# A table of single moves on top of a planned instruction order, in a fused hash-masked attention and mixture-of-attention kernel

## The chip, the cores and the metric

The kernel runs on one core of a Trainium2 chip. The metric is the device time of one execution in microseconds (us), as the median over the runs of the kernel. Beside these runs one execution was recorded by the hardware profiler; its span is the time from its first to its last instruction.

## The reference, cut to what matters

Two stages follow each other. The first is an attention over 4 batches, 8 heads, 768 tokens and 64 dimensions, in which a query sees only the keys whose six sign bits (the signs of a projection) are its own. The second is a mixture of four causal attention heads over the first stage's output, with the two largest gate logits of a token as its weights.

```python
q_bits = (np.einsum('bhsd,dk->bhsk', q, proj) > 0); k_bits = (np.einsum('bhsd,dk->bhsk', k, proj) > 0)
mask = q_bucket[:, :, :, None] == k_bucket[:, :, None, :]
scores = np.where(mask, scale * np.matmul(q, k.transpose(0, 1, 3, 2)), -1e9)
attn = np.exp(scores - np.max(scores, -1, keepdims=True))
x = np.matmul(attn / (np.sum(attn, -1, keepdims=True) + 1e-09), v)      # -> [4, 768, 512]
logits = x @ w_gate                                                     # top 2 of 4, softmax over the two
for e in range(4):                                                      # q = x @ wq[e], k = x @ wk[e], v = x @ wv[e]
    scores = np.where(causal, -1e9, scale * (q @ k.transpose(0, 2, 1)))
    a = softmax(scores)
    out += weight_of_e * (a @ v @ wo[e])
```

## The kernel before

The work consists of 48 units: 32 heads of the first stage (each batch has 8) and 16 of the second (4 for each batch). A unit goes through the same steps each time. `max_steps` multiplies queries and keys on TensorE into tiles named `mx`, and VectorE reduces each to row maxima (`pm`; `pmw` for the first four heads, which use a wider fp32 path). `shift_steps` turns the maxima into a row that is put under the queries by a DMA: `negm` or `negh` on VectorE, a transposition into `misc` on TensorE, then a copy `roww` or `row`, and for the hash heads `fr`, which a DMA puts into `fq`. `s_unit` then goes over pieces of 128 keys by up to 512 queries: `qk` multiplies into `st` (two matmuls a tile) and ScalarE takes the exponential twice, as fp32 `p32` (`p` in the profile's rows) and as fp16 `ph`; `lo` takes `pl` = `p32` - `ph` on GpSimd; `av` multiplies `ph` by `vh`, `ph` by `vl` and `pl` by `vh` into `o`. At the end of a hash head three or more matmuls `o<-vs,fq` close the sum, and `normalise` divides it (`rden`, its reciprocal, `xp`). `prep_v` makes `vf` and `vh` on ScalarE and `vl` on GpSimd, and adds up columns of them with matmuls `misc<-ones,vh` and `misc<-ones,vl`. Other jobs load inputs, find signs and scales, split operands into two fp16 parts (the instructions SCALAR_TENSOR_TENSOR `qk<-natq` and `qk<-natk` on VectorE), project for the second stage and write the output.

Buffers are rings: three PSUM tiles `st`, two `mx`, two `misc`, one `o`; four `p32`, seven `ph`, five `pl`. A tile is used again when its readers are through.

No instruction is issued where it is written. A recorder notes all 10,944 operations with what each depends on; `schedule` then places them one by one on their engines, by planned durations (`TIMES`), latencies and priorities (a table `PLACE` shifts the priority of each job on each engine). In the planned waits of TensorE during the opening it sets dummy matmuls `o<-ident`. `issue` issues the list in its order: each engine carries out its own instructions in the order in which they were issued, and waits by semaphores for what the next one needs. An operation may have two alternatives (a copy on ScalarE or VectorE). A field `after` gives a GpSimd operation one wait more, for a VectorE operation on which it does not depend; `schedule` sets it where the plan has both at the same time. All instructions of the profile thus carry one line number, that of the call in `issue` (L735).

Of the kernel before, what the change touches and what calls it, by code (L numbers as in the profile page):

```python
# [141 lines left out]
LAT = {"tensor": 55.0, "scalar": 36.0, "vector": 37.0, "gpsimd": 78.0, "sync": 28.0}  # L142
LAT2 = {"tensor": 55.0, "scalar": 103.0, "vector": 100.0, "gpsimd": 132.0, "sync": 28.0}
LAT_PE = {"gpsimd": 174.0}


PLACE = [
# [315 lines left out]
class Recorder:  # L463
# [103 lines left out]
    def schedule(self):  # L567
# [14 lines left out]
        def after(p, e, many):  # L582
            if p.eng == e:
                return p.end + SAME[e]
            return p.end + (LAT_PE[e] if e in LAT_PE and many and p.eng == "tensor" else (LAT2 if many else LAT)[e])

# [15 lines left out]
        order = []  # L602
# [8 lines left out]
        while left:  # L611
# [41 lines left out]
            st, o, a, pen = best  # L653
# [66 lines left out]
                    enter(p)  # L720
            order.append((o, a))
        self.length = max(o.end for o in self.ops)
        return order

    def issue(self):
        def real(x):
# [1201 lines left out]
```

## Time and profile before

| | before |
|---|---|
| median of 3 runs | 605.97 us (605.92 to 608.73) |
| the profiled execution, its own time | 606.81 us |
| its span | 605.0 us |
| mean granted clock of TensorE | 0.999 of full speed |
| instructions | 20,583 |

The page names the engines PE (TensorE), PEld (its weight loads, which overlap PE), DVE (VectorE), ACT (ScalarE), POOL (GpSimd) and SP (the engine that issues most DMAs). Matmuls overlap each other: a row's duration is that of one matmul from start to end, while the next may start much earlier. A busy engine is therefore not the same as an engine at its peak. Idle time stands in brackets in a row, with the instruction that ended it.

### The profile page before, as it was taken

What the parts mean: (1) busy time and instruction counts of PE and PEld (TensorE: products, weight loads), DVE (VectorE), ACT (ScalarE), POOL (GpSimd) and SP (SyncE); (2) the same over time, 40 slices, a digit from 0 to 9 for tenths busy, and PEclk for the clock granted to TensorE, in tenths of its full rate; (3) what the DMA queues carried; (4) which work ended last, traced back from release to release, by engine and by line L of the source; (5) the groups of instructions that cost most, each with busy time, mean ns of one, the idle gap of its engine ahead of it and who ended that gap; (6) DMA issues with size and microseconds to landing.
All of it is one profiled execution on the core that took longest, in us unless ns stands there. A gap on an engine that the chain in (4) does not pass through costs nothing.

```text
span 605.0 us, 20583 instructions
## 1 busy us (share of the span) xinstructions
PE 591.0 (98%) x7911; PEld 434.0 (72%) x7911; DVE 503.2 (83%) x1383; ACT 497.6 (82%) x1060; POOL 465.6 (77%) x520
## 2 busy tenths in 40 slices
PE   8999999999999999999999999999999999999996
PEld 7677876767777677777766777777776677776673
DVE  5899979999879898977979988888998967557753
ACT  6588999999679998968988798976987997943783
POOL 9478898999658899867895889974894889931740
PEclk9999999999999999999999999999999999999999
DMA  6564053141320433131234224123051210002222
GB/s 183 141 190 126 9 167 110 43 149 40 107 61 16 143 91 76 36 113 28 94 102 133 83 47 120 29 95 72 20 165 73 76 29 23 10 1 64 62 89 105
DMA packets 32921, 50.26 MB, mean 83 GB/s; under 512 B 6411, under 2 KB 20535, under 8 KB 32823
## 3 DMA queue, kind: packets, MB, share of 16 engines
q1 hardware_dynamic: 32810, 48.95, 28.0%
q8 instruction: 62, 1.02, 0.7%
q14 instruction: 37, 0.29, 0.2%
q10 hardware_dynamic: 12, 0.00, 0.0%
HBM read 20.98 MB, written 6.29 MB: 45 GB/s over the span
## 4 chain that ended last, share of the span: by engine, by line
PE 82%; ACT 8%; DVE 3%; POOL 2%; issue 2%; DMA 1%; SPq 0%; ACTq 0%; DVEq 0%; POOLq 0%
PE misc L735 24%; PE st L735 24%; PE o L735 22%; PE mx L735 12%; ACT ph L735 3%; ACT p L735 3%; POOL pl L735 2%; DVE pm L735 1%; DVE qk L735 1%; DMA qk<-qk 1%; DMA wst<-in_wvg_dram 1%; ACT vf L735 0%; ACT qk L735 0%; DVE xt L735 0%; POOL vl L735 0%
## 5 line engine op out<-in xcount | busy, mean ns | idle before, releaser
L735 POOL TENSOR_TENSOR pl<-p,ph 128x512 f16<-128x512 f32 x367 | 411.2, 1148 | 115.5 <-ACT ph L735 49.7
L735 ACT ACTIVATE p<-st 128x512 f32<-128x512 f32 x372 | 225.7, 608 | 34.8 <-PE st L735 28.3
L735 PE MATMUL st<-qk 78*128 78x512 f16 (+3 forms) x976 | 228.1, 323 | 1.0 <-ACT ph L735 0.7
L735 ACT ACTIVATE ph<-st 128x512 f16<-128x512 f32 x372 | 224.1, 611 | 2.3 <-PE o L735 2.0
L735 DVE TENSOR_REDUCE pm<-mx 128x2 f32<-128x512 f32 (+2 forms) x284 | 186.0, 675 | 16.9 <-PE mx L735 15.2
L735 PEld LDWEIGHTS <-ph 128*128 128x128 f16 x2880 | 160.2, 98 | 24.6 <-issue 1.0
L735 PEld LDWEIGHTS <-qk 78*128 78x128 f16 (+5 forms) x1560 | 129.5, 98 | 55.2 <-issue 5.3
L735 PEld LDWEIGHTS <-pl 128*128 128x128 f16 x1440 | 133.1, 97 | 10.5 <-POOL pl L735 2.2
L735 PE MATMUL mx<-qk 76*128 76x512 f16 (+2 forms) x488 | 134.7, 323 | 2.4 <-DVE pm L735 1.1
L735 PE MATMUL o<-vh,ph 128*128 128x65 f16 x1104 | 128.9, 195 | 0.3 <-DVE xp L735 0.2
L735 PE MATMUL o<-vl,ph 128*128 128x64 f16 x1104 | 128.3, 193 | 0.8 <-POOL vl L735 0.8
L735 PE MATMUL o<-vh,pl 128*128 128x65 f16 x1104 | 128.3, 194 | 0.1
L735 PE MATMUL misc<-xt,wqk_h 128*128 128x384 f16 x256 | 57.7, 325 | 0.3 <-DVE qk L735 0.3
L735 DVE CUSTOM_DVE_ANT_0 spare<-mx,causal 128x512 bf16<-128x512 f32 (+2 forms) x96 | 44.3, 461 | 6.4 <-PE mx L735 4.1
L735 PEld LDWEIGHTS <-xt 128*128 128x128 f16 x324 | 30.5, 97 | 11.2 <-ACT xt L735 0.5
L735 PE MATMUL o<-mvh,pl 128*128 128x65 f16 x336 | 37.6, 193 | 0.5 <-POOL pl L735 0.5
L735 PE MATMUL o<-mvh,ph 128*128 128x65 f16 x336 | 37.6, 194 | 0.0
L735 PE MATMUL o<-mvl,ph 128*128 128x64 f16 x336 | 37.5, 192 | 0.0
L735 POOL TENSOR_TENSOR vl<-vf,vh 128x384 f16<-128x384 f32 x32 | 30.1, 948 | 7.0 <-ACT vh L735 3.5
L735 PEld LDWEIGHTS <-wqk_h 128*128 128x128 f16 x256 | 23.9, 98 | 14.2 <-issue 0.7
L735 PE MATMUL misc<-xt,wqk_l 128*128 128x384 f16 x128 | 29.9, 325 | 0.0
L735 PE MATMUL misc<-wvg_h,xt 128*128 128x260 f16 x192 | 29.4, 274 | 0.0
(198 smaller groups left out, 890.9 us busy)
## 6 DMA issues: line engine op xcount, KB each, us to landing
qk<-qk SPq DMA_DIRECT2D x128, 96.0 KB
natv<-in_v_dram SPq DMA_DIRECT2D x16, 384.0 KB
qk<-qk SPq DMA_DIRECT2D x32, 192.0 KB
natq<-in_q_dram SPq DMA_DIRECT2D x15, 384.0 KB
natk<-in_k_dram SPq DMA_DIRECT2D x15, 384.0 KB
out_dram<-ot SPq DMA_DIRECT2D x20, 256.0 KB
wst<-in_wqk_dram SPq DMA_DIRECT2D x4, 256.0 KB
xt<-xt SPq DMA_DIRECT2D x4, 192.0 KB
```

The costliest lines, as they stand in the source:

```text
L735: o.made = getattr(getattr(self.nc, e), m)(*[real(x) for x in args], **{k: real(x) for k, x in kw.items()})
```

## The change

The changed kernel has three tables more and a method `moved`, through which `schedule` sends its finished list. `MOVES` has 3,501 entries `i:p`: operation `i` is taken out of its place and put right behind operation `p`. `SWAPS` lists 37 operations which take their other alternative: 23 copies go from VectorE to ScalarE, 13 from ScalarE to VectorE, and one `pl` from VectorE to GpSimd. One of them stands in the first 127 us, the copy `vr` at 49.47 us. `BEHIND` replaces the planner's own 27 `after` waits of GpSimd by 21 others. The operations themselves, the tiles, the rings and the dummy matmuls are the same.

```diff
+MOVES = """
+5:9 13:5 17:13 15:17 2:6 18:8 20:12 19:14 23:22 66:30 31:66 43:31 134:33 3:134
...
+SWAPS = (481, 2075, 2308, 2255, 2459, 2523, 3066, 4379, 4559, 4645, 4807, 4875, 4887, 4938, 5410, 5695, 6259, 6468, 6894, 6835, 7064, 7531, 7599, 8248, 9032, 8
...
+BEHIND = """
+797:372 386:388 935:833 1105:863 2002:1776 2043:1806 2509:2511 2786:2559 3279:3227 3429:3238 5012:4507 4654:4523 5261:5252 5368:5263
...
@@ -720,7 +980,41 @@
         self.length = max(o.end for o in self.ops)
-        return order
+        return self.moved(order)
+
+    def moved(self, order):
+        first, at = {}, {}
+        for x in MOVES.split():
+            i, p = map(int, x.split(":"))
+            at[p] = i
+        gone = set(at.values())
+        swaps = set(SWAPS)
+        for o in self.ops:
+            o.after = None
+        for x in BEHIND.split():
+            i, p = map(int, x.split(":"))
+            self.ops[i].after = self.ops[p]
+        for o, a in order:
+            if o.i >= 0 and o not in first:
+                first[o] = a
+        ops = {o.i: (o, next(b for b in o.alts if b is not a) if o.i in swaps else a) for o, a in first.items()}
+        out, seen, p = [], set(), -1
+        while p in at:
+            p = at[p]
+            out.append(ops[p])
+        for o, a in order:
+            if o.i < 0 or o.i in seen:
+                out.append((o, a))
+                continue
+            seen.add(o.i)
+            if o.i in gone:
+                continue
+            p = o.i
+            out.append(ops[p])
+            while p in at:
+                p = at[p]
+                out.append(ops[p])
+        return out
```

Most moves are short. On TensorE 1,584 of 7,643 operations leave the order in which they stood to each other, nine in ten of its operations stand within 9 places of where they stood, and the first 20 us of its program are as before. On VectorE 186 operations leave that order, on ScalarE 305, on GpSimd 84 and on SP 114. Three places follow. The first is VectorE's program from about 9 to 22 us, around the first head's maxima (`pmw`), its `fr`, and the four sign instructions `xt<-misc,least_times` of the first head pair. Before:

```order
L735 TENSOR_REDUCE pmw_183<-mx 128x2 x9
L735 TENSOR_REDUCE negm_163<-pmw_183 128x12
L735 TENSOR_SCALAR fr<-misc 12x128
L735 TENSOR_SCALAR xt<-misc,least_times 13x384 x2
L735 TENSOR_SCALAR xt<-misc,least_times 12x384 x2
L735 TENSOR_REDUCE mx<-pst 128x1
L735 TENSOR_REDUCE mx<-natv 128x1
```

The same stretch of VectorE's program after the change:

```order
L1029 TENSOR_REDUCE pmw_172<-mx 128x2 x8
L1029 TENSOR_REDUCE mx<-pst 128x1
L1029 TENSOR_REDUCE pmw_172<-mx 128x2
L1029 TENSOR_REDUCE negm_147<-pmw_172 128x12
L1029 TENSOR_SCALAR xt<-misc,least_times 12x384
L1029 TENSOR_SCALAR xt<-misc,least_times 13x384 x2
L1029 TENSOR_SCALAR xt<-misc,least_times 12x384
L1029 TENSOR_SCALAR fr<-misc 12x128
L1029 TENSOR_REDUCE mx<-natv 128x1
```

The four sign instructions now stand ahead of `fr`, and `mx<-pst` stands further up. On SP's queue the DMA `fq<-fr` stays ahead of a load of `natv` and of two weight loads, which change places with each other behind it.

The second place is GpSimd's program from about 40 to 49 us, with the pair of `vl` that belongs to the next head (`x2`) and the `pl` around it. Before:

```order
L735 TENSOR_TENSOR vl_718<-vf_265,vh_257 128x6x64
L735 TENSOR_TENSOR pl<-p_915,ph 128x512
L735 TENSOR_TENSOR pl<-p_929,ph 128x512
L735 TENSOR_TENSOR pl<-p_943,ph 128x512
L735 TENSOR_TENSOR vl_981<-vf_268,vh_260 128x6x64 x2
L735 TENSOR_TENSOR pl<-p_1005,ph 128x512
```

After the change (buffer numbers differ, since tiles are numbered in the order of issue):

```order
L1029 TENSOR_TENSOR vl_703<-vf_261,vh_270 128x6x64
L1029 TENSOR_TENSOR pl<-p_919,ph 128x512
L1029 TENSOR_TENSOR pl<-p_931,ph 128x512
L1029 TENSOR_TENSOR vl_980<-vf_170,vh_197 128x6x64 x2
L1029 TENSOR_TENSOR pl<-p_945,ph 128x512
L1029 TENSOR_TENSOR pl<-p_992,ph 128x512
```

The pair of `vl` now stands ahead of the third `pl`.

The third place is VectorE's program from about 47 to 52 us, between the end of a head (`rden` to `xp`) and a maximum over a weight tile (`qkmax<-wst`). Before:

```order
L735 TENSOR_REDUCE pmw_185<-mx 128x2 x2
L735 TENSOR_SCALAR rden<-o,cs_590 128x6
L735 TENSOR_REDUCE qkmax<-wst 128x2
L735 RECIPROCAL rden<-rden 128x6
L735 TENSOR_TENSOR vr_235<-misc,vr_235 1x128
L735 TENSOR_TENSOR xp<-o,rden 128x6x64
L735 TENSOR_REDUCE pmw_185<-mx 128x2 x2
```

And after the change:

```order
L1029 TENSOR_REDUCE pmw_176<-mx 128x2 x2
L1029 TENSOR_SCALAR rden<-o,cs_590 128x6
L1029 CAST vr_257<-misc 1x128
L1029 RECIPROCAL rden<-rden 128x6
L1029 TENSOR_TENSOR vr_257<-misc,vr_257 1x128
L1029 TENSOR_TENSOR xp<-o,rden 128x6x64
L1029 TENSOR_REDUCE pmw_176<-mx 128x2 x2
L1029 TENSOR_REDUCE mqk<-natq 128x1
L1029 TENSOR_REDUCE mqk<-natk 128x1
L1029 TENSOR_REDUCE pmw_176<-mx 128x2
L1029 TENSOR_REDUCE qkmax<-wst 128x2
```

`qkmax<-wst` has gone behind `xp` and five other reductions; the copy `vr`, one of the 37, has come over from ScalarE.

## Rows read from the trace of the kernel before

**Rows 1.** The page: busy time and share of each engine; shares of the last chain.

```profile
PE 591.0 (98%) x7911; PEld 434.0 (72%) x7911; DVE 503.2 (83%) x1383; ACT 497.6 (82%) x1060; POOL 465.6 (77%) x520
...
PE 82%; ACT 8%; DVE 3%; POOL 2%; issue 2%; DMA 1%; SPq 0%; ACTq 0%; DVEq 0%; POOLq 0%
```

**Rows 2.** Windows: stretch and length, busy us (instructions) per engine, clock, DMA share, GB/s.

```profile
0.00:50.00 50.00, 45.11 (x492) 35.13 (x493) 40.22 (x87) 34.86 (x78) 36.27 (x113) 1.00 0.60 173
50.00:100.00 50.00, 48.58 (x714) 37.86 (x713) 45.70 (x108) 46.90 (x98) 44.77 (x40) 1.00 0.32 97
```

**Rows 3.** Windows again, one stretch of 20 us; engines PE, PEld, DVE, ACT, POOL.

```profile
80.00:100.00 20.00, 19.08 (x262) 13.79 (x260) 19.26 (x41) 20.00 (x43) 18.09 (x18) 1.00 0.49 159
```

**Rows 4.** Timeline of PE: start, duration, form, count, idle time before and its releaser.

```profile
1.83 0.61 PE L735 MATMUL o<-ident 128*128 128x128 bf16 x4 [1.83 <-DVE ident L735]
...
17.20 2.40 PE L735 MATMUL o<-ident 128*128 128x128 bf16 x40
20.21 0.70 PE L735 MATMUL mx<-xt 76*128 76x512 f32 x3 [0.62 <-DVE xt L735]
...
46.53 0.27 PE L735 MATMUL o<-vs,fq 80*128 80x65 f16 x3
47.66 0.18 PE L735 MATMUL misc<-ones,vl 128*128 128x1 f16 x1 [0.86 <-POOL vl L735]
...
50.62 0.19 PE L735 MATMUL o<-vh,ph 128*128 128x65 f16 x1 [0.22 <-DVE xp L735]
...
61.69 0.38 PE L735 MATMUL st<-qk 77*128 77x256 f32 x1 [0.19 <-ACT ph L735]
...
89.23 0.38 PE L735 MATMUL st<-qk 78*128 78x512 f16 x1 [0.16 <-ACT ph L735]
...
399.67 0.32 PE L735 MATMUL mx<-qk 65*128 65x384 f16 x1 [0.46 <-DVE pm L735]
...
554.87 0.59 PE L735 MATMUL mx<-qk 65*128 65x512 f16 x2 [1.04 <-DMA qk<-qk]
...
600.33 0.38 PE L735 MATMUL o<-wo_h,xt 128*128 128x512 f16 x1
```

**Rows 5.** Timeline of DVE at the three places and at one split of keys.

```profile
17.70 0.28 DVE L735 TENSOR_SCALAR fr<-misc 12x128 f16<-12x128 f32 x1 [1.50 <-ACT roww L735]
18.01 2.76 DVE L735 TENSOR_SCALAR xt<-misc,least_times 13x384 fp32r<-13x384 f32 x4
...
43.81 1.00 DVE L735 SCALAR_TENSOR_TENSOR qk<-natk,cs,qk 128x768 f16<-128x768 f32 x1
...
48.38 1.21 DVE L735 TENSOR_REDUCE qkmax<-wst 128x2 f32<-128x1024 f32 x1
...
50.03 0.53 DVE L735 TENSOR_TENSOR xp<-o,rden 128x384 f32<-128x384 f32 x1
...
64.47 1.25 DVE L735 SCALAR_TENSOR_TENSOR qk<-natq,cs,qk 128x768 f16<-128x768 f32 x1
```

**Rows 6.** Timeline of ACT and of SP's queue at the first and second place.

```profile
44.31 0.97 ACT L735 ACTIVATE vh<-vf 128x384 f16<-128x384 f32 x2
...
18.00 0.77 SPq L735 DMA_DIRECT2D fq<-fr  x1
18.83 0.41 SPq L735 DMA_DIRECT2D natv<-in_v_dram  x1
```

**Rows 7.** Timeline of POOL at the second place, and beside the split of rows 5.

```profile
41.57 4.26 POOL L735 TENSOR_TENSOR pl<-p,ph 128x512 f16<-128x512 f32 x3 [0.38 <-ACT ph L735]
45.80 1.81 POOL L735 TENSOR_TENSOR vl<-vf,vh 128x384 f16<-128x384 f32 x2
...
63.75 2.99 POOL L735 TENSOR_TENSOR pl<-p,ph 128x512 f16<-128x512 f32 x2
```

**Rows 8.** Waits up to 100 us: who, for whom, total us, times, longest.

```profile
PEld st L735 <- ACT ph L735: 2.3, 7, 0.6
```

**Rows 9.** The page's costliest groups: the subtraction on POOL, with its mean in ns.

```profile
L735 POOL TENSOR_TENSOR pl<-p,ph 128x512 f16<-128x512 f32 x367 | 411.2, 1148 | 115.5 <-ACT ph L735 49.7
```

More of the change, by code (lines that the diff above doesn't have):

```diff
@@ L144 @@
 LAT_PE = {"gpsimd": 174.0}
+MOVES = """
[251 rows of a table added]
+"""
+SWAPS = (481, 2075, 2308, 2255, 2459, 2523, 3066, 4379, 4559, 4645, 4807, 4875, 4887, 4938, 5410, 5695, 6259, 6468, 6894, 6835, 7064, 7531, 7599, 8248, 9032, 8772, 9351, 10196, 9912, 10354, 10381, 10472, 10697, 10786, 10907, 10912, 10942,)
+BEHIND = """
+797:372 386:388 935:833 1105:863 2002:1776 2043:1806 2509:2511 2786:2559 3279:3227 3429:3238 5012:4507 4654:4523 5261:5252 5368:5263
+5955:5959 6610:6596 6684:6612 7463:7247 8438:7976 8679:8726 10786:10780
+"""
 PLACE = [
```

250 rows, old and new, of the table MOVES are left out of this document.

## Prediction

> **What bounds the kernel now.** I read the page first, then windows, then PE's timeline, and last the engines that PE waits for. PE is busy 591.0 us of a span of 605.0, and the chain that ended last is PE for 82% of it [rows 1]. No work is removed, and nearly all that is moved keeps its engine, so the change can only win time in which PE stands still, or in which two matmuls follow each other later than they could.
>
> Two bounds for that. The windows give the time without any matmul: 4.89 us in the first 50 us and 1.42 in the next 50 [rows 2]; over the whole span it is 605.0 - 591.0 = 14.0 [rows 1]. Of it 1.83 lies before the first matmul, which waits for VectorE's `ident`, and some 4.3 behind the last, which starts at 600.33 and takes 0.38 [rows 4]; the change leaves both parts alone. So 7.9 us are idle inside. The busy column hides more, since matmuls overlap: a matmul that starts 0.2 us late is covered by the end of the one before. I therefore took the distance from each matmul's start to the next one's, for all 7911 from 1.83 to 600.33 [rows 4], less the median distance of the same shape: 166 of them are over 0.04 us too long, 24.8 us in sum. 13 are over 0.4 us (8.6 us together), the other 153 add up to 16.2, of which 11.1 lie in the first 100 us.
>
> **The change part by part.** The sum is made against the profiled execution's 606.81 us, that is the span and 1.81 around it; the median of the runs, 605.97, is 0.84 lower, and I take that off at the end.
>
> *First place, PE's 0.62 us ahead of 20.21.* PE runs dummies from 17.20 for 2.40 us, to 19.60, and then waits for VectorE's signs [rows 4]. VectorE has nothing to do for 1.50 us before `fr`, which waits for ScalarE's `roww`; the four signs stand behind `fr` and run from 18.01 for 2.76 us [rows 5]. Now they stand ahead. They can begin at 17.70 - 1.50 = 16.20 at the earliest, and at 17.70 at the latest; three of them take about 2.07, so PE can go on between 18.3 and 19.8, where it is free at 19.60. Gain 0.62, at least 0.4; more is not there, as the dummies stay. What is late next: `fr` by some 2 us, and with it the DMA `fq<-fr`, at 18.00 on SP's queue, and `natv` behind it at 18.83 [rows 6], which the weight loads also pass. `fq` is first read at 46.53 [rows 4], the head pair's `vh` comes at 44.31 [rows 6]: over 20 us of cover, so nothing.
>
> *Second place, 0.86 us ahead of 47.66.* PE's `misc<-ones,vl` waits for the pair of `vl` [rows 4], which GpSimd starts at 45.80, after three `pl` from 41.57 to 45.83 [rows 7]. ScalarE's two `vh` are ready at about 44.8 and 45.28 [rows 6]. With only two `pl` ahead (2 of 1.15 us [rows 9], to about 43.9) the pair begins at 44.8 and is done 1.81 later, at 46.6 to 46.7. PE comes there right after 46.53 and its two steps, at 46.66. All 0.86 goes; if the signs' 0.62 makes PE come earlier but not `vh`, as little as 0.4 does. The third `pl` ends at about 47.9 in place of 45.8, still ahead of the `o` matmuls from 50.62 [rows 4].
>
> *Third place, 0.22 us ahead of 50.62.* PE waits for `xp` [rows 4]; `qkmax` (1.21 us) ran before it [rows 5] and now comes after, while the copy `vr` comes in between. A copy of one row I take at the 0.28 of `fr` [rows 5]. So `xp` is some 0.9 earlier and the 0.22 goes (0 if `rden`'s own input is the limit).
>
> *Small named ones.* Ahead of 61.69 and 89.23 PE waits 0.19 and 0.16 for ScalarE's `ph` [rows 4]; its program has now a matmul that was ready in front of each: 0.35 (0 to 0.35). Ahead of 399.67 it waits 0.46 for a maximum on VectorE [rows 4], which has moved up a little: 0.26 (0 to 0.46).
>
> *What stays.* The 1.04 us before 554.87 is a chain of a copy, a DMA and its landing [rows 4], whose order is the same.
>
> *The 153 small steps.* Those named above take 1.0 of their 16.2 us. Of the other 15 I take a fifth as gone, 3.0, because about a fifth of PE's operations (1,584 of 7,643) change places with neighbours; bounds 0, as a neighbour need not be ready earlier, and 7.5, half of it. Against that a moved matmul can meet an operand that is not ready where it was ready before. I take 1.0 for that, three such waits at the mean of 2.3 / 7 = 0.33 us [rows 8]; bounds 0 and the second rival's 10.5.
>
> *The copies and GpSimd's waits.* Only one copy of the 37 is in the first 127 us; later ACT and DVE have spare time (82% and 83% busy [rows 1]). Nothing. Five of the 21 waits put a `pl` behind a split of VectorE that ran beside it. The row at 64.47 shows what the overlap costs: the split takes 1.25 us where another took 1.00 [rows 5], and the two `pl` beside it 2.99 [rows 7] where two take 2.30 [rows 9]. A `pl` that waits for the split ends at about 65.5 + 1.15 = 66.65 and not at 63.75 + 2.99 = 66.74. So the wait is worth 0 to 0.1 on GpSimd and 0.25 on VectorE, and I count nothing, for PE waits for neither there.
>
> The Trainium skill (SBUF — State Buffer, section "Who interferes with whom") says that a VectorE instruction with two SBUF inputs and a GpSimd one that reads SBUF exclude each other, that the loser is fully blocked, and that issue order decides who it is. By that the five waits of this kind would give back nothing on either engine, and the sum below would stand as it is. By the rows both lose a little, and five times 0.25, if all of it lay on the path, would make the sum 1.25 us lower. The trace agrees with the page on the blocked `pl` and not on the split, which by the page should have kept its 1.00 us.
>
> **Sum.** 0.62 + 0.86 + 0.22 + 0.35 + 0.26 = 2.31 named; 3.0 - 1.0 = 2.0 from the small steps; 606.81 - 4.31 = 602.5, and in terms of the median 601.7. With all lower bounds of the gains it would be 605.2 before new waits, with all upper ones 596.
>
> **Rivals.**
> 1. *What is won early is waited for later.* From 80 to 100 us ACT is busy 20.00 us of 20, DVE 19.26, POOL 18.09 [rows 3]. If these engines give the pace there, PE arrives earlier and waits longer, and all that was won up to then is returned. What remains is 0.26 and a fifth of the 5.1 us of small steps behind 100 us, less 0.3 for new waits: 605.97 - 1.0 = 605.0. For it: ACT has no gap left. Against it: PE too is at 19.08 of 20 there, and starts that stretch with tiles ahead of it.
> 2. *Slower: moved matmuls wait.* PE takes its instructions in order, so one that is moved ahead of its operand stops all behind it. The leads in PE's program are short because three `st` tiles go round. If one in fifty of the 1,584 waits 0.33 us [rows 8], that is 10.5 us: 605.97 - 5.3 + 10.5 = 611. It cancels the gains at 16 such waits and is measurably slower from 25 on. For it: of the small steps only 5.1 us lie in the 500 us behind 100, so over most of the span there is more to break than to mend. Against it: the moves are short, within 9 places for most.
> 3. *Much faster.* If the moves close most of the 7.9 us of inner idle time and a part of the covered steps, it ends at 605.97 - 7.9 = 598 or a little below. For it: 11.1 of the 16.2 us lie in 100 us where many operations stand elsewhere. Against it: the waits on GpSimd and on DMAs stay in their order.
>
> **How the numbers follow.** The sum's case, 599.5 to 603.5, has a chance of 0.45; the first rival, 603.5 to 607, 0.24; the second, above 607, 0.16; the third, below 599.5, 0.15. A measurement of this kernel tells about 0.5% from no change, 3.0 us. Faster than 602.9 are the third rival and all but 0.04 of the sum's case: 0.56. Slower than 609.0 is put at the whole second rival, 0.16, and the rest, 0.28, is no change. The range reaches from 596, the sum's upper bounds, to 608, which leaves out a little of the third rival and most of the second. The likeliest case's own range is 599.5 to 603.5.
>
> **What would show it.** In the profile after: no idle time before PE's first `mx<-xt` (now 20.21) and the four signs ahead of `fr`; the pair of `vl` done when PE comes to `misc<-ones,vl`; no wait for `xp` at some 49 us; PE at 46.4 or more of the first 50 us and the busy sums of DVE, ACT and POOL as before, within 1%. The first rival would show as more waits of PE for `ph` between 70 and 130 us; the second as many new waits of 0.2 to 0.5 us for `ph`, `pm` or `pl` behind 100 us. The prediction is wrong if PE's small late starts go in far larger number than a fifth, or if the leads that the moves use up were needed.

## The result and the profile after

The changed kernel takes 615.31 us (median of 4 runs, 613.01 to 617.84), the kernel before 606.22 in the same measurement: a ratio of 1.013 with an interval of 1.010 to 1.0165. It is slower by some 9 us, and the prediction, 601.7 with a range up to 608, was wrong in sign.

Runs in which TensorE's mean granted clock is lower take longer, so "whole clock" below means a clock of 0.9985 or more: of the four runs of after two took 613.0 and 613.1 us at 0.994 and 0.993 and two 617.5 and 617.8 at 0.988, and of 29 runs of the kernel before in one measurement 20 took 605.8 at whole clock and 9 took 608.6 (medians).

The profiled execution of after is the one of 613.01 us, with a span of 611.2, against 606.81 and 605.0 before. Its rows thus account for 6.2 of the 9 us; no profile here shows what the two runs of 617 us lost beside that.

The page's busy times after, in the columns of [rows 1], and its chain:

```profile
PE 596.1 (98%) x7911; PEld 437.0 (71%) x7911; DVE 511.9 (84%) x1372; ACT 501.1 (82%) x1070; POOL 464.1 (76%) x521
...
PE 89%; DVE 6%; DMA 2%; issue 1%; ACT 0%; POOL 0%; DVEq 0%; POOLq 0%
```

PE is busy 5.1 us longer with the same 7911 matmuls, and VectorE 8.7 us longer with 11 instructions fewer. More busy time for less work means instructions that were held up or ran slower. The windows say where (columns as in [rows 2]); first after, then before:

```profile
96.00:100.00 4.00, 3.89 (x61) 2.97 (x58) 4.00 (x1) 4.00 (x10) 4.00 (x5) 1.00 0.51 164
100.00:104.00 4.00, 1.05 (x6) 0.38 (x6) 4.00 (x3) 1.76 (x4) 3.65 (x4) 0.76 0.33 132
104.00:108.00 4.00, 2.79 (x27) 2.00 (x27) 4.00 (x9) 0.00 (x0) 1.05 (x1) 0.50 0.21 52
108.00:112.00 4.00, 4.00 (x50) 2.61 (x49) 2.70 (x9) 3.51 (x7) 2.55 (x3) 0.88 0.21 48
```

```profile
100.00:104.00 4.00, 3.69 (x59) 2.61 (x57) 4.00 (x8) 3.64 (x9) 4.00 (x4) 1.00 0.41 125
104.00:108.00 4.00, 4.00 (x71) 3.14 (x68) 4.00 (x15) 4.00 (x10) 4.00 (x5) 1.00 0.32 75
```

Between 100 and 108 us PE carries out 33 matmuls in place of 130. It is idle for 4.2 us, and the granted clock in the same windows is 0.76, then 0.50: half speed, 1.2 GHz, for 6.8 us from 102.1 us on, when PE had just waited 1.49 us and was waiting again. VectorE counts as busy all the time, with a single instruction between 96 and 100 us. Its timeline after, at that place:

```profile
95.89 5.45 DVE L1029 SCALAR_TENSOR_TENSOR qk<-natq,cs,qk 128x768 f16<-128x768 f32 x1
101.25 1.90 DVE L1029 SCALAR_TENSOR_TENSOR qk<-natk,cs,qk 128x768 f16<-128x768 f32 x1
103.08 1.21 DVE L1029 TENSOR_REDUCE mw<-wst 128x1 bf16<-128x1024 f32 x1
104.21 0.27 DVE L1029 TENSOR_TENSOR vr<-misc,vr 1x128 f16<-1x128 f32 x1
104.41 0.15 DVE L1029 TENSOR_REDUCE mw<-wst 128x1 bf16<-128x16 f32 x1
104.48 1.27 DVE L1029 TENSOR_REDUCE pm<-mx 128x2 f32<-128x512 f32 x2
```

A split that takes 1.0 to 1.25 us elsewhere [rows 5] takes 5.45. What GpSimd does meanwhile, after:

```profile
92.65 7.86 POOL L1029 TENSOR_TENSOR pl<-p,ph 128x512 f16<-128x512 f32 x7
100.86 1.48 POOL L1029 TENSOR_TENSOR pl<-p,ph 128x512 f16<-128x512 f32 x1 [0.35 <-ACT p L1029]
```

Seven subtractions without a gap, to 100.51; in the first gap behind them (0.35 us) the split gets through. And PE's three waits after:

```profile
101.38 0.32 PE L1029 MATMUL misc<-qk,pbh 128*32 128x384 f16 x1 [1.49 <-DVE qk L1029]
103.21 0.51 PE L1029 MATMUL misc<-qk,pbh 128*32 128x384 f16 x3 [1.51 <-DVE qk L1029]
...
105.20 0.58 PE L1029 MATMUL mx<-qk 76*128 76x512 f16 x1 [1.26 <-DVE pm L1029]
```

In the kernel before, the same place reads so on VectorE and on GpSimd:

```profile
96.54 2.19 DVE L735 SCALAR_TENSOR_TENSOR qk<-natq,cs,qk 128x768 f16<-128x768 f32 x1
98.65 1.00 DVE L735 SCALAR_TENSOR_TENSOR qk<-natk,cs,qk 128x768 f16<-128x768 f32 x1
```

```profile
93.38 4.54 POOL L735 TENSOR_TENSOR pl<-p,ph 128x512 f16<-128x512 f32 x4
99.83 3.38 POOL L735 TENSOR_TENSOR pl<-p,ph 128x512 f16<-128x512 f32 x3 [1.91 <-ACT vf L735]
```

GpSimd paused for 1.91 us at 97.9. The row puts this down to ScalarE's `vf`; it was one of the planner's `after` waits, subtraction 1567 behind VectorE's split `natk` (operation 1339). The new table `BEHIND` has no such entry. Of the 27 waits before, six, all behind splits, have no successor in it, and this is one.

To see the whole span I compared the start of each matmul with the start of the same one before (medians of stretches, us late, before's time):

```text
kernel            14-18  46-48  57-60  75-80  93-98  108-112  130-140  235-245  545-551  590-601
after              0.13  -1.54  -0.37   0.29   0.20     6.28     6.61     7.58     7.27     6.69
```

It wins 1.7 us up to 47 us, as the first two places should, loses 1.8 again by 80 us, 6.1 at 100 us and 1.3 between 112 and 245. Such a row compares two single executions, and these scatter: the first run below has the same order up to 95 us and is 2.0 us late there, not 0.2. A step at one place tells more than a delay. The gain behind 550 us is no effect of the change: two runs further down whose order there is that of before have it too.

### The profile page after: what moved, and what is told of

The parts are those of the page before. It is cut to its first block, busy times and chain, and to the rows that moved or that the text cites. A ratio compares the mean times of both kernels' runs of the same rounds, so it can differ in the third digit from the quotient of the medians.

```text
span 611.2 us, 20400 instructions
## 1 busy us (share of the span) xinstructions
PE 596.1 (98%) x7911; PEld 437.0 (71%) x7911; DVE 511.9 (84%) x1372; ACT 501.1 (82%) x1070; POOL 464.1 (76%) x521
## 4 chain that ended last, share of the span: by engine, by line
PE 89%; DVE 6%; DMA 2%; issue 1%; ACT 0%; POOL 0%; DVEq 0%; POOLq 0%
PE st L1029 27%; PE misc L1029 25%; PE o L1029 25%; PE mx L1029 13%; DVE qk L1029 2%; DVE pm L1029 1%; DVE pmw L1029 1%; DMA qk<-roww 1%; DMA natk<-in_k_dram 1%; DVE spare L1029 0%; DMA qk<-row 0%; DVE xt L1029 0%; DVE misc L1029 0%; DVE xp L1029 0%; POOL pl L1029 0%
## 5 line engine op out<-in xcount | busy, mean ns | idle before, releaser
L1029 PE MATMUL st<-qk 78*128 78x512 f16 (+5 forms) x976 | 255.1, 325 | 1.1 <-DMA qk<-roww 0.7
L1029 ACT ACTIVATE ph<-st 128x512 f16<-128x512 f32 x372 | 216.4, 605 | 20.5 <-PE st L1029 16.7
L1029 ACT ACTIVATE p<-st 128x512 f32<-128x512 f32 x372 | 217.6, 607 | 16.1 <-PE st L1029 7.9
L1029 PEld LDWEIGHTS <-ph 128*128 128x128 f16 x2880 | 184.6, 98 | 41.1 <-issue 3.5
L1029 PEld LDWEIGHTS <-qk 128*128 128x128 f16 (+5 forms) x1560 | 130.1, 99 | 43.1 <-issue 5.2
L1029 PE MATMUL o<-vh,pl 128*128 128x65 f16 x1104 | 155.9, 194 | 0.1
L1029 PE MATMUL o<-vh,ph 128*128 128x65 f16 x1104 | 155.8, 195 | 0.2
L1029 PE MATMUL o<-vl,ph 128*128 128x64 f16 x1104 | 154.8, 193 | 0.8 <-POOL vl L1029 0.8
L1029 PE MATMUL mx<-qk 76*128 76x512 f16 (+2 forms) x488 | 143.3, 325 | 2.3 <-DVE pm L1029 2.1
L1029 PE MATMUL o<-mvh,ph 128*128 128x65 f16 x336 | 44.2, 193 | 0.0
```

Of the source, the lines that this page charges most:

```text
L1029: o.made = getattr(getattr(self.nc, e), m)(*[real(x) for x in args], **{k: real(x) for k, x in kw.items()})
```

## Experiments

Theory A: the dropped wait starves VectorE's split, PE stalls for it, and its clock falls. Rival B: VectorE's own moved instructions make that stall. Rival C: many small new waits of moved instructions, all over the span.

All times are medians beside runs of the kernel before on the same chip, with the ratio to it and its interval; for differences under 1% the median at whole clock is given too where it matters.

**One wait put back** (in the changed kernel):

```diff
 BEHIND = """
-5955:5959 6610:6596 6684:6612 7463:7247 8438:7976 8679:8726 10786:10780
+5955:5959 6610:6596 6684:6612 7463:7247 8438:7976 8679:8726 10786:10780 1567:1339
```

> The changed kernel with one GpSimd wait of the kernel before put back: the subtraction 1567 waits for VectorE's split 1339 (natk). Theory A (without that wait GpSimd's subtractions follow each other without a gap, VectorE's split natq at 95.9 us is kept from its operands for 5.4 us, PE stands still for some 4 us, and its clock falls to half for 6.8 us): the split takes about 2 us again, no stretch with a granted clock below 1, and the time falls by the 6 us that the stretch of 95 to 105 us costs, to 605.5 to 608. Theory B (the moves of VectorE's own instructions at about 100 us make the stall, above all a maximum of 1.2 us that now stands ahead of two that PE waits for): the stall and the low clock stay, 611 to 618. Theory C (many small new waits all over the span): 611 to 613, hardly changed.

610.77 us, 1.0059 (1.0037 to 1.0081). The clock stays whole in the profiled run, the two waits of PE for the splits are gone from its rows, and the step at 100 us is 1.3 us (1.99 late at 93 to 98, 3.26 at 108 to 112) in place of 6.1. So some 4.5 of the 9 us hang on this one wait; neither A alone (605.5 to 608) nor B or C alone (611 or more) gives 610.8. Left at this place is one wait of PE, and what VectorE does ahead of it:

```profile
103.85 0.38 PE L1029 MATMUL mx<-qk 76*128 76x512 f16 x1 [1.49 <-DVE pm L1029]
```

```profile
97.68 3.20 DVE L1029 SCALAR_TENSOR_TENSOR qk<-natq,cs,qk 128x768 f16<-128x768 f32 x1
100.80 1.00 DVE L1029 SCALAR_TENSOR_TENSOR qk<-natk,cs,qk 128x768 f16<-128x768 f32 x1
101.73 1.21 DVE L1029 TENSOR_REDUCE mw<-wst 128x1 bf16<-128x1024 f32 x1
```

**The same wait taken from the kernel before:**

```diff
         self.length = max(o.end for o in self.ops)
+        self.ops[1567].after = None
         return order
```

> The kernel before with that one wait (1567 on 1339) taken away and nothing else; the two operations share no data, so nothing in the result depends on it. Theory A: the split natq takes 4 us or more, PE stops for 3 us or more at about 100 us, the clock falls to half for a while, and the time is 610 to 614. Theories B and C: as before, 605.5 to 607.

612.53 us, 1.0102 (1.0069 to 1.0136): theory A. Its start times against before are the cleanest of all: 0.88 us late at 93 to 98 us, 6.20 at 108 to 112, 5.95 at 545. One semaphore wait, on which no data hang, is worth 5.3 us at this place, the fall of the clock included. Its VectorE and GpSimd:

```profile
97.42 5.51 DVE L736 SCALAR_TENSOR_TENSOR qk<-natq,cs,qk 128x768 f16<-128x768 f32 x1
```

```profile
93.16 8.95 POOL L736 TENSOR_TENSOR pl<-p,ph 128x512 f16<-128x512 f32 x8
```

**Only the moves of the first 60 us** (planner's waits kept, 240 moves, one copy):

```diff
+MOVES = """
+5:9 13:5 17:13 15:17 2:6 18:8 20:12 19:14 23:22 66:30 31:66 43:31 134:33 3:134 46:24 68:37
...
+SWAPS = (481,)
```

> The kernel before with only those moves whose operations both stand in the first 60 us or so of the order (240 moves), and the one swapped copy there; the planner's own 27 waits kept. The prediction's terms for the three places (0.62, 0.86, 0.22) would make it 604.3 to 604.9. The first rival of the prediction (what is won early is waited for later) makes it 605.5 to 606.5, the same as before. Theories A to C say nothing of it but that the clock stays whole.

606.49 us, 0.9989 (0.997 to 1.0008); with whole clock 605.5 against 606.1. More than half of the 1.2 to 1.8 us expected is given back, and the profile shows one place: PE now stops for a DMA. In its profiled run the clock falls there too (0.51 from 48 to 52 us).

```profile
48.80 0.77 PE L793 MATMUL st<-qk 77*128 77x512 f32 x1 [0.80 <-DMA qk<-roww]
```

**Dummies in the stall of the changed kernel**, to part the clock from the stall:

```diff
+        for i, n in ((1380, 30), (1381, 30), (1525, 24)):
+            k = next(k for k, (o, a) in enumerate(out) if o.i == i)
+            c = next(o.outs[0].tile for o, a in out[k - 1::-1] if a[0] == "tensor" and o.i >= 0 and o.outs[0].tile.name.startswith("o"))
+            out[k:k] = [(warm, self.spare[c])] * n
         return out
```

> The changed kernel with 84 dummy matmuls (about 0.05 us each) on PE ahead of the three instructions that wait at 99.6 to 105.2 us; nothing else changed. If PE's idle time is what makes the clock fall, the clock stays whole, and the time is that of the changed kernel without the loss by the clock: about 2 to 3.5 us less than its 613.0, so 609.5 to 611. If the clock falls for another reason, there is a stretch at half clock as before and the time is 613 or more.

613.25 us, 1.0101 (1.0072 to 1.0129): the time is missed by 2 us, the clock was as expected. The window row has PE busy and the clock whole where after has 1.05 and 0.76:

```profile
100.00:104.00 4.00, 3.97 (x76) 3.39 (x73) 4.00 (x3) 1.96 (x5) 3.64 (x3) 1.00 0.45 159
```

So it is PE's idle time that drops the clock here. What that costs is less than I expected: from 93-98 to 108-112 us this kernel loses 4.45 us, the changed one 6.08, so the half clock is worth some 1.6 us at this place and the stall itself 4.4. In the changed kernel PE has only 36 matmuls in the 6.8 us at half speed and stands idle for 2.4 of them:

```profile
102.10:108.93 6.83, 4.46 (x36) 2.66 (x36) 6.29 (x10) 0.79 (x2) 2.95 (x3) 0.50 0.14 34
```

At the end even the 1.6 us are not seen any more: the two profiled executions have spans of 611.0 and 611.2.

**The other moves, by stretch of the order** (planner's waits kept; 213, 899, 1615 and 520 moves):

```diff
+MOVES = """
+742:741 448:742 743:832 941:743 744:449 933:450 845:894 1878:943 958:944 959:834 846:945 963:951 847
...
+SWAPS = ()
```

> The kernel before with only the 213 moves between about 62 and 113 us of its order; the planner's 27 waits kept, no copy swapped. Theory A (the dropped wait makes the large step at 100 us) and theory B (VectorE's own moves there add to it: the maximum over a weight tile, 1.21 us, now stands behind both splits and ahead of the maxima that PE waits for): the split natq takes 2 to 3.3 us, PE waits 1 to 1.5 us for `pm` at about 102 us, and the time is 0.8 to 1.5 us above before. If theory B holds nothing, it is within 0.3 us of before.

> The kernel before with only the 899 moves and 8 swapped copies between about 113 and 250 us; the planner's waits kept. Theory C (moved matmuls now wait a little, in many places): a handful of new waits of 0.2 to 0.6 us between 120 and 210 us, together 1.0 to 1.8 us above before. If the drift there comes from the changed waits or from what happened at 100 us: within 0.4 us of before.

> The kernel before with only the 1615 moves and 17 swapped copies between about 250 and 500 us; the planner's waits kept. Between 260 and 500 us the changed kernel drifts by only some 0.2 us against the one before, so half of all moves should give within 0.5 us of before. If the prediction's term for the small steps were right, it would be 1 us or more below before.

> The kernel before with only the 520 moves and 11 swapped copies behind 500 us; the planner's waits kept. The wait for a DMA of 1.04 us at 554 us, which the prediction left unchanged, is half as long in the changed kernel: 0.8 to 1.2 us below before. If that gain hung on what came earlier: as before.

```text
moves of       median   ratio (interval)            whole clock, before   growth of the delay in the stretch
62 - 113 us    608.58   1.0033 (1.0013 to 1.0053)   607.98, 606.05        3.29 -> 4.70
113 - 250 us   608.51   1.0038 (1.0018 to 1.0058)   607.60, 606.05        -0.65 -> 0.93
250 - 500 us   608.27   1.0021 (1.0002 to 1.0041)   606.81, 606.05        -0.51 -> 0.42 (at 550 us)
500 - 605 us   607.19   1.0002 (0.9982 to 1.0022)   606.02, 606.05        3.08 -> 2.61
```

(Whole clock: 4, 6, 5 and 7 of 12 runs.) Three of the four stretches lose, none wins. Only the second came out as expected, at whole clock; the first and the third lost more, and the last did not win. 14 of the 3,501 moves cross the borders of the stretches and are in none of these runs. The last stretch's wait for a DMA at 554 us is shorter, but so it is in the runs of 113 to 250 and of 250 to 500 us, whose order there is that of before (the delay falls by 0.8 and 1.2 us): that wait varies by itself. For the second stretch the chain of small new waits is seen in PE's waits between 113 and 250 us, where before has only the 0.5 for `pl`:

```profile
PE o L835 <- POOL pl L835: 0.4, 1, 0.4
PE misc L835 <- DVE xt L835: 0.4, 1, 0.4
PE misc L835 <- DVE mvl L835: 0.3, 1, 0.3
PE st L835 <- DMA qk<-row: 0.2, 1, 0.2
```

**The maximum left in its place** (in the run of 62 to 113 us):

```diff
-... 1592:1611 1132:1339 1571:1132 1734:1571
+... 1592:1611 1571:1339 1734:1571
```

> The 62 to 113 us moves as in the run of that stretch alone, but the maximum over a weight tile (1.21 us) stays where it was, ahead of the two splits. Theory B (it is this maximum, in front of the two that PE waits for, that makes the step at 102 us): PE's wait for `pm` there is 0.5 us or less, as before, and the time is 0.6 to 1.3 us below that run, some 0.3 to 0.9 above before. If the other 212 moves make the step: the same as that run.

607.70 us, 1.0019 (1.0000 to 1.0039); whole clock 606.92, that is 1.13 above before on its chip, against 1.93 with the maximum moved (607.98 on another chip). PE's longest wait for `pm` at the place is 0.2 us in place of 1.1. The single move thus costs about 0.8 us (4 runs at whole clock on either side): theory B holds for it, as a second cause beside A. The other 212 moves still cost about 1 us. In this profiled run the clock was at half from 94.8 to 98.2 us, behind waits of PE of only 0.22 and 0.41 us (3.44 busy of the 4 from 92 us on), so a fall does not need a stall as long as that of the changed kernel.

**The row first** (in the run of the first 60 us):

```diff
-... 457:456 454:457 422:426
+... 457:456 422:426
-... 590:551 453:455 591:514
+... 590:551 591:514
```

> The moves of the first 60 us without the two that put `roww` and its DMA behind `fr`, `fq<-fr` and a load of `natq`. If the late row is what eats the gain of the three places: no wait of PE for the DMA `qk<-roww` at 48 us, a time 1.0 to 1.8 us below before where the clock is whole, and fewer runs with a lower clock than before has. If something else eats it (rival 1 of the prediction): as before, within 0.6.

605.73 us, 0.9986 (0.997 to 1.0002); whole clock 605.19 against 605.79, less than the 1.0 expected, and no more at whole clock than without this mend (605.46 against 606.09). The wait for the DMA is gone, and none of its 11 runs has a clock under 0.997, where 7 of the 29 of before have 0.996 or less. But of 1.9 us won by 47 us 1.06 are given back by 60. What takes that back I did not settle; it is no single wait in PE's rows. The first rival of the prediction is not it: it saw the gain returned between 80 and 100 us, and there the lead stays as it is (0.83 us at 57 to 60, 0.85 at 93 to 98, 0.93 at 545).

**No GpSimd waits at all** (in the kernel before):

```diff
+        for o in self.ops:
+            o.after = None
         return order
```

> The kernel before without any of the planner's 27 GpSimd waits; no data hang on them. Theory A in general (a split of VectorE gets no turn while GpSimd's subtractions follow each other without a gap): several of the 28 splits take 2 to 6 us, and the time is 612 to 620. If the place at 96 us is the only one where it matters: 611 to 613, as with the one wait taken away. If waits cost as much as they bring elsewhere: below 611.

613.75 us, 1.0113 (1.0082 to 1.0144), hardly more than without the one. Six of the 28 splits lengthen by 0.6 us or more, only the one at 99.58 by more than 1 us (it takes 5.53). What the other 26 waits are worth together is less than these intervals can tell. Its profiled run has two falls of the clock, here and at 48 us, and a mean clock of 0.989.

```profile
48.00:52.00 4.00, 3.90 (x24) 3.12 (x25) 3.15 (x8) 2.26 (x7) 1.16 (x2) 0.56 0.39 138
...
106.00:110.00 4.00, 3.11 (x25) 1.87 (x25) 3.97 (x8) 0.00 (x0) 1.72 (x1) 0.56 0.16 41
```

**The head with the row first and one wait more:**

```diff
-5368:5263 5955:5959 6000:6002 6610:6596 6713:6612 7412:7231 7463:7247 8438:7976 8122:7987 8679:8726 10811:10786
+5368:5263 5955:5959 6000:6002 6610:6596 6713:6612 7412:7231 7463:7247 8438:7976 8122:7987 8679:8726 10811:10786 1533:1309
```

> The head moves with the row first, and one wait more than the planner had: the subtraction 1533 waits for the split natq (1309), which takes 2.2 us in the kernel before. Theory A: the split takes about 1.0 us, the wait of PE for `pm` at 100 us (0.31) goes, and the time is 0.2 to 0.6 us below the run without this wait. If the wait only moves the delay to GpSimd, which PE then waits for: the same or up to 1 us more.

604.46 us, 0.9972 (0.9957 to 0.9987): the one version whose interval lies below the kernel before. The split takes 1.07 us, and GpSimd pauses earlier and shorter than the 1.91 before:

```profile
95.79 1.07 DVE L793 SCALAR_TENSOR_TENSOR qk<-natq,cs,qk 128x768 f16<-128x768 f32 x1
```

```profile
97.03 5.13 POOL L793 TENSOR_TENSOR pl<-p,ph 128x512 f16<-128x512 f32 x4 [0.99 <-DVE qk L793]
```

**The changed kernel mended**: both waits, the maximum and the row put back.

```diff
-... 1132:1339 1571:1132
+... 1571:1339
-... 457:456 454:457
+... 457:456
-... 453:455 591:514
+... 591:514
-... 8679:8726 10786:10780
+... 8679:8726 10786:10780 1567:1339 1533:1309
```

> The changed kernel with three mends: the wait 1567 on 1339 back and 1533 on 1309 added, the maximum over the weight tile back ahead of the splits, `roww` and its DMA back ahead of `fq<-fr`. If the causes add up as the single runs show them: 610.8 (with the one wait back) less 1.1 for the maximum, 0.8 for the row and 1.0 for the further wait, so 607 to 608.5, still 1 to 2 us above before, which is the drift behind 113 us. If a cause not yet named holds much of the loss: 609.5 or more. If the three were all: 604 to 606.

607.49 us, 1.0008 (0.9988 to 1.0027), inside the sum that was expected, and no run under 0.997 of clock. So these mends together take away the loss but for about 1.3 us at whole clock (607.43 against 606.14), and the profiled run shows the drift behind 113 us: 0.79 early at 108 to 112 us, 0.78 late at 235 to 245. That the single terms add up is not shown by this: the further wait by itself is worth less than its 1.0 (next run), the maximum some 0.8 and not 1.1, and the row nothing at whole clock.

**The further wait alone** (in the kernel before):

```diff
+        self.ops[1533].after = self.ops[1309]
         return order
```

> The kernel before with the one wait more (1533 on the split 1309) and nothing else. Theory A: the split takes about 1.0 us in place of 2.2, and the time is 0.5 to 1.2 us below before. If the gain of the run with the head moves hung on these: within 0.3 of before.

606.40 us, 1.0002 (0.9984 to 1.0020). The split takes 1.05 us, so the mechanism works, but the median shows no gain. Its starts say why: 0.17 us early at 93 to 98 us, 0.91 at 100 to 104, but 0.48 at 108 to 112, so some 0.4 of 0.7 us is given back at once. The run of the head with this wait has the same pattern (0.75, 1.50, 1.05). So the 1.3 us between the two runs of the head is not explained by the wait alone.

**The moves of 113 to 250 us without their copies:**

```diff
-SWAPS = (2075,2308,2255,2459,2523,3066,4379,4559,)
+SWAPS = ()
```

> The 899 moves between about 113 and 250 us without the 8 copies that change engines there. If the moves make the drift: 1.2 to 1.8 us above before, as with the copies. If the copies make it (seven of them add to ScalarE's work): within 0.4 us of before.

609.47 us, 1.0043 (1.0022 to 1.0063), 2.9 above before at whole clock and so more than the 1.2 to 1.8 expected. In the stretch itself the delay grows by 1.8 us (0.67 to 2.45), as against 1.6 with the copies: the drift there is the moves' and not the copies'. The rest of the 2.9 us is not explained.

## Why the prediction was wrong, step by step

*The copies and GpSimd's waits, "I count nothing".* This step failed, and with some 5 us it is the largest. The prediction looked at waits that the new table has, singled out five of them behind a split, and priced each by what an overlap costs, 0 to 0.1 us on GpSimd and 0.25 on VectorE. It did not look at the six that are gone. A wait that GpSimd sits out for 1.91 us looks like a loss on GpSimd; it was the pause in which VectorE's split got through, and PE waited for the split. Taking it from the kernel before alone costs 5.3 us at the place.

The Trainium skill (SBUF — State Buffer, "Who interferes with whom") was cited there for the rule that issue order decides who is blocked. By the rule as I read it, a split loses at most the `pl` that runs when it is issued. The row that the prediction took for a disagreement agrees with that: the split at 64.47 [rows 5] was issued while a `pl` ran (63.75 [rows 7] to 64.91), it ended 0.81 us behind that one, and it was the next `pl` that was kept, for 1.88 us:

```profile
64.86 1.88 POOL L735 TENSOR_TENSOR pl<-p,ph 128x512 f16<-128x512 f32 x1
```

At six more places of the kernel before a split goes ahead of the next `pl` in this way, though that follows without a gap. The split `natq` at 96 us is the one that a `pl` passed over. That of after was issued at 95.89, ahead of the four `pl` that began at 96.00 to 99.34, and still came behind all of them, to 100.51. The trace of before had the sign already: its split was issued at 96.54, and the `pl` begun at 96.73 went ahead of it until 97.92; its 2.19 us are the longest of the 28 splits there. Why this one is passed over is not shown. It need not be: in the run of the moves of 62 to 113 us it was issued earlier within a `pl` (0.71 us before its end, not 0.15 to 0.27) and got its turn, with the next `pl` kept for it:

```profile
99.84 1.53 DVE L792 SCALAR_TENSOR_TENSOR qk<-natq,cs,qk 128x768 f16<-128x768 f32 x1
```

```profile
100.52 1.87 POOL L792 TENSOR_TENSOR pl<-p,ph 128x512 f16<-128x512 f32 x1
```

Over all 17 traces every split that was passed over had been issued in the last 0.27 us of a subtraction, and it then came behind each further `pl` that followed without a gap; but not every split issued so late was passed over.

*The 153 small steps, "3.0 gone, 1.0 for new waits".* The sign was wrong. With the planner's waits kept, the moves of 62 to 113, 113 to 250 and 250 to 500 us lose about 1.9, 1.55 and 0.8 us at whole clock, 4.2 together in place of a gain of 2.0. Of the first, some 0.8 is a single instruction, the maximum of 1.21 us put between the splits and the `pm` that PE waits for. A fifth of the places changed is no measure of a gain: in these runs the moves cost more than they closed.

*The three places* were right in mechanism at the first two. PE has no idle time ahead of its first `mx<-xt`, nor ahead of `misc<-ones,vl`, and starts are 1.54 us earlier by 47 us, where 0.62 + 0.86 = 1.48 was forecast. After:

```profile
17.33 2.40 PE L1029 MATMUL o<-ident 128*128 128x128 bf16 x40
19.53 0.60 PE L1029 MATMUL mx<-xt 76*128 76x512 f32 x2
...
46.08 0.18 PE L1029 MATMUL misc<-ones,vl 128*128 128x1 f16 x1
...
48.47 0.47 PE L1029 MATMUL st<-qk 77*128 77x512 f32 x1 [0.70 <-DMA qk<-roww]
```

At the third place the 0.22 for `xp` went and 0.70 for a DMA came. The prediction followed `fr` and SP's queue at the first place and not here, where the same pair has changed places: the row's DMA now stands behind `fq<-fr` and a load. SP's queue after:

```profile
42.79 0.68 SPq L1029 DMA_DIRECT2D fq<-fr  x1
43.59 0.33 SPq L1029 DMA_DIRECT2D natq<-in_q_dram  x1
44.03 0.76 SPq L1029 DMA_DIRECT2D qk<-roww  x1
```

*The rivals.* The first had the early gain returned, and it was, by 80 us; but its place, 80 to 100 us, and its cause, engines without a gap, are not what the runs show. The second, moved matmuls that wait, was right for behind 113 us, with 2 to 3 us and not 10.5. The place of the largest loss was in none of them, and no rival had PE's clock in it: all sums ran at one speed. The profile of before, with the clock at 1.00 in the windows shown, does not tell how near a stall like that at 100 us, or one of about 1 us at 48 us in some runs, is to a fall; runs beside it do. The Trainium skill (TensorE: Matmul & The Clock Gate, "What's actually happening") says that the clock hangs on how busy PE has been; the run with dummies agrees, with the clock at 1.00 where PE was kept busy and at 0.76 and 0.50 in the two windows of after where it was idle for 2.95 and 1.21 of 4 us.

## What to carry to other kernels

A wait that costs its own engine time may be what gives another engine its turn: before a scheduler's waits are set anew, list those that are gone, not only those that are new, and look at who runs beside them. On an engine that is 98% busy, moves of instructions have little to win and much to lose; test them by stretch, since 240 of 3,501 moves, less two and with one wait more, gave the only gain here. When a step is taken ahead of another, follow its queue at each place where the same pair stands, not only at the first.

## Not expected of the hardware

- A split on VectorE with two SBUF operands that is passed over at the end of one GpSimd subtraction `pl` came behind each further `pl` of a series without a gap: it took 5.45, 5.51 and 5.53 us where four more went ahead of it, 2.19 where one did, and 1.05 to 1.07 where a wait stopped GpSimd first. Most splits are not passed over; then the next `pl` is kept and takes 1.87 us or so in place of 1.15.
- The fall of PE's clock to half for 6.8 us, within a stall of about 4 us, cost 1.6 us at the place, less than the stall.
- The kernel before sits near such a fall itself: the stall of 0.86 us at 47.66 [rows 4] lies where a profiled run with its order up to 500 us (that of the last stretch's moves) fell to half clock (0.55 from 48 to 52 us) and was 2.6 us late afterwards. In the mended kernel, which has no such stall, none of 12 runs was below 0.997.
